# Zeroing the spare columns of VM earlier on GpSimd, in the prologue of a fused attention and mixer kernel

## The chip, the cores and the metric

The kernel runs on one core of one Trainium2 chip. The metric is device microseconds from start to end of one execution. A profile's span is some 1.8 us shorter than that time, because it counts from the first to the last instruction. Where two kernels are compared, they ran in turns on the same chip.

## The reference, cut to what matters

```python
x = A_x                                     # [1, 2048, 512] bf16
xn = _layernorm(x, axis=-1)
return x + _A_ref(xn, A_wqkv, A_wo) + _B_ref(xn, B_w1, B_b1, B_w2, B_b2)
# A: attention with 32 heads of 16; B: layer norm, token-mixing MLP, F = 1376
```

Only the first microseconds matter here. The layer norms of the first four token tiles (128 tokens each) must be done before the first scores can be computed, and all the rest follows.

## The kernel before

A list scheduler written in Python lays out every instruction of the five engines before the program is built. GpSimd ("pool") has several small jobs in the prologue. It takes the reciprocal root of each tile's variance, which VectorE ("dve") needs for the tile's layer norm, and it zeroes the columns of V and of VM (V scaled by a constant) that a later read touches beyond the written ones.

```python
def zero_memsets(nm, whole, kh):            # three of 128x256, one of 128x16
    for T in range(1, 4):
        sc.add("pool", lambda e, T=T: e.memset(kh[:, :, 8 * T, 0:16], 0.0), ...)
    sc.add("pool", lambda e: e.memset(whole[:, NKT * H * 17:], 0.0), ...)

def ln_rstd(t, n):                          # GpSimd: add epsilon, then power -1/2
    sc.add("pool", lambda e: e.tensor_scalar(mv[:, t:t + n, 3], mv[:, t:t + n, 1], EPS, None, ALU.add), ...)
    sc.add("pool", lambda e: e.tensor_tensor(mv[:, t:t + n, 2], ..., ALU.pow), ...)

def ln_norm(t):                             # VectorE: (x - mean) * root, bf16 to bf16
    sc.add(..., lambda e: e.tensor_scalar(xn_sb[:, t, :], x_sb[:, t, :], mv[:, t, 0:1], mv[:, t, 2:3],
                                          ALU.subtract, ALU.mult), ...)
# ... the prologue, in order:
zero_memsets("V", V17, v17_kh)
ln_sums(1)
warm_up(N_WARM, 5)                          # 13 matmuls that open TensorE's clock
ln_stats(0)
# ... statistics of tiles 1 and 2
ln_rstd(1, 2)
ln_norm(0)
ln_stats(3)                                 # ends with the root of tile 3 on GpSimd
for t in range(1, NPRE):
    ln_norm(t)
zero_memsets("VM", VM, vm_kh)               # on GpSimd: right behind the root of tile 3
# ... then TensorE transposes the normed tiles 0 to 3, projects Q and K, and scores begin
```

The softmax here doesn't subtract the row's maximum and nothing guards it: scores larger than these inputs give would overflow.

Of the kernel before, what the change touches and what calls it, by code (L numbers as in the profile page):

```python
# [52 lines left out]
SEM = 0.05  # L53
PE_SWITCH = 0.10
PER_LIST = 16
SEG = 8
RULES = (
    (0.5, 0.5, 0.3, 0.0, 6, 0),
    (0.3, 0.5, 0.3, 0.0, 6, 0),
# [6 lines left out]
    (0.5, 0.5, 0.3, 0.0, 4, 6),  # L66
    (0.5, 0.8, 0.45, 0.1, 4, -6),
)
RULE_OF = "00008220310000100058660800426859400150020974970367941473943140809177076731670813606801617338009600085119008766223163090020510000"
LN2_AT = 12  # L70
PIECE_OPEN = 1
HOLD_MAX = 2.0
ZERO_AT = 4
POOL_NORM = ()
STATS_LEAD = 0
N_LAST = 0
# [283 lines left out]
def bass_parallel_sum__softmax_full_mha__mixer_token_mlp__prompt_kernel(  # L360
# [18 lines left out]
    with ExitStack() as es:  # L379
        block = es.enter_context(nc.Block())  # L380

        def sb(name, shape, dt):
            return es.enter_context(nc.sbuf_tensor(name, shape, dt))
# [20 lines left out]
        VM = sb("VM", [128, NKT * H * 17 + 16], BF16)  # L404
# [37 lines left out]
        def bank(i):  # L442
            return ps[:, i * 512:(i + 1) * 512]
# [26 lines left out]
        vm_kh = VM[:, 0:NKT * H * 17].rearrange("p (k h c) -> p k h c", k=NKT, c=17)  # L470
# [8 lines left out]
        def zero_memsets(nm, whole, kh):  # L479
            for T in range(1, 4):  # L480
                sc.add("pool", lambda e, T=T: e.memset(kh[:, :, 8 * T, 0:16], 0.0),
                       writes=[(nm, t, T) for t in range(NT)], cost=(0.3, 0.4))
            sc.add("pool", lambda e: e.memset(whole[:, NKT * H * 17:], 0.0), writes=[(nm, NKT, 0)], cost=(0.1, 0.2))
# [56 lines left out]
        def ln_stats(t):  # L540
            sc.add("dve", lambda e: e.bn_stats(stats[:, t, :], x_sb[:, t, :]),
                   reads=[("x", t)], writes=[("stats", t)], cost=(0.6, 0.69))
            sc.add("dve", lambda e: e.bn_aggr(mv[:, t, 0:2], stats[:, t, :]),
                   reads=[("stats", t)], writes=[("mv", t)], cost=(0.12, 0.18))
            ln_rstd(t, 1)
# [8 lines left out]
        def ln_sums(t):  # L554

            for fn, col in ((ACTF.Identity, 3), (ACTF.Square, 1)):
                sc.add("act", lambda e, fn=fn, col=col: e.activation(xn_sb[:, t, :], x_sb[:, t, :], fn,
                                                                    accum_out=mv[:, t, col:col + 1]),
                       reads=[("x", t)], writes=[("xn", t), ("mv", t)], cost=(0.55, 0.7))
# [10 lines left out]
        def ln_norm(t):  # L570
            pool = t in POOL_NORM
            sc.add("pool" if pool else "dve", lambda e: e.tensor_scalar(xn_sb[:, t, :], x_sb[:, t, :], mv[:, t, 0:1], mv[:, t, 2:3],
                                                    ALU.subtract, ALU.mult),
                   reads=[("x", t), ("mv", t)], writes=[("xn", t)], cost=(2.09, 2.2) if pool else (0.3, 0.39), port=pool)
# [92 lines left out]
        def warm_up(n, bk, src=pT[:, NPB - 1, 0:512], keys=(("pT", NPB - 1),)):  # L667
            for _ in range(n):
                sc.add("pe", lambda e: e.matmul(bank(bk), lhsT=src[:, 0:128], rhs=src, start=True, stop=True),  # L669
                       reads=keys, writes=[("bank", bk)], cost=("F", (0, 1, 2, 3), 0.3), name="warm")  # L670

        sc.add("act", lambda e: e.activation(rcomp[:, 0, 0:1], mhalf[:], ACTF.Exp), reads=[("mhalf",)],
               writes=[("rcomp", 0)], cost=(1.4, 1.5))
        zero_memsets("V", V17, v17_kh)
        ln_sums(1)
        warm_up(N_WARM, 5)
        ln_stats(0)
# [5 lines left out]
        ln_stats(3)  # L683
        for t in range(1, NPRE):
            ln_norm(t)
        zero_memsets("VM", VM, vm_kh)

        TB = (0, 1, 2, 3)
        for t in range(NPRE):
# [18 lines left out]
        for half in (1, 0):  # L708
            cs = slice(256 * half, 256 * half + 256)
            sc.add("dve", lambda e, half=half, cs=cs: e.tensor_scalar(QT[:, 1, cs], bank(QB[half])[:, cs], qmask[:, 1:2], None, ALU.mult),  # L710
                   reads=[("bank", QB[half]), ("qmask",)], writes=[("QT", 1, r) for r in range(4)], cost=(0.35, 0.42))
        ln_norm(NPRE)
        for t in range(NPRE + 1, NPRE + 1 + STATS_LEAD):
            ln_stats(t)

        def zero_wo_t():
            dma("sp", wo_t[:], QT[:, 3:4, :].to_broadcast([128, 4, 512]),
                reads=[("QT", 3, r) for r in range(4)], writes=[("wo_t", z) for z in range(4)], name="zero")

        def block0_work(period):  # L720
            if period == ZERO_AT:
                zero_wo_t()
            if period == 0:
                for t in range(NPRE):
                    vt_tile_pe(t, 0, 5, t)
                vt_evac(list(range(NPRE)), 0, 5, "dve")

            def ok(t):
                return NPRE <= t < NT

            if ok(period + 2):
                transpose_copy(period + 2, 4, "dve")
            if ok(period + 1):
                kt_tile_evac(0, period + 1, EX_BANK, "dve")
            if ok(period) and period % 2 == 0:
                vt_evac([period, period + 1], 0, 5, "dve")
            if period == 1:
                warm_up(5, PV_BANK, KT[:, 0, 0:512], [("KTt", 0, z) for z in range(4)])
            if NKT - 2 <= period < PER_LIST:
                warm_up(3, 4, KT[:, 0, 0:512], [("KTt", 0, z) for z in range(4)])  # L740
            if ok(period + 3):
                transpose_pe(period + 3, 4)
            if ok(period + 2):
                kt_tile_pe(0, period + 2, EX_BANK)
                vt_tile_pe(period + 2, 0, 5, period % 2)
            if ok(period + 5 + STATS_LEAD):
                ln_stats(period + 5 + STATS_LEAD)
            if ok(period + 5) and period + 5 in POOL_NORM:
                ln_norm(period + 5)
            if ok(period + 4) and period and period + 4 not in POOL_NORM:  # L750
                ln_norm(period + 4)
            if period == 1:
                sc.add("pool", lambda e: e.memset(QT[:, 2:4, :], 0.0),
                       writes=[("QT", i, r) for i in (2, 3) for r in range(4)], cost=(0.9, 1.0))
# [644 lines left out]
        while True:  # L1399
            D_LATE, D_BACK, D_STEAL, PAIR_WAIT, piece_min, LATE_BY = RULES[int(RULE_OF[min(next_n, NN - 1) // SEG])]  # L1400
            cands = []
# [294 lines left out]
```

## Time and profile before

| | before |
|---|---|
| time, median of the first 3 runs | 684.36 us (684.14 to 684.39) |
| span of the profile | 682.6 us |
| TensorE / ScalarE busy | 98% / 98% |
| VectorE / GpSimd busy | 90% / 61% |
| norm of tile 3 on VectorE | 0.92 us, the other fifteen about 0.4 |
| first exponential on ScalarE | 11.33 us |

The lines behind this table stand in the prediction. Below, "norm 3" is VectorE's layer norm of token tile 3, and "load" is TensorE's weight load (PEld in the profile). In the profile's lines, x8 stands for eight instructions in one row, and a bracket tells how long the engine was idle before, and whose work ended that.

### The profile page before, as it was taken

The numbers are of one execution on the slowest core, as the hardware profiler recorded it, in microseconds if no ns is written. First come the engines' busy times: TensorE is split into PE (matmuls) and PEld (weight loads), VectorE is DVE, ScalarE is ACT, GpSimd is POOL, SyncE is SP. The second block draws the span as 40 slices with busy tenths as digits, with TensorE's granted clock in tenths as the row PEclk, the third lists the DMA queues.
The fourth block names the chain that finished last, engine by engine and source line by source line (L and its number), as shares of the span: only waits on it lengthen the run. The fifth ranks groups of instructions, "written<-read, shape, count | busy, mean of one in ns | idle before, by whom it ended". The sixth has DMA issues, their size and how long they took to land.

```text
span 682.6 us, 29520 instructions
## 1 busy us (share of the span) xinstructions
PE 670.7 (98%) x12969; PEld 312.4 (46%) x12972; DVE 617.0 (90%) x882; ACT 667.7 (98%) x731; POOL 417.6 (61%) x717
## 2 busy tenths in 40 slices
PE   8999999999999999999999999999999999999997
PEld 4534544445444445444444444444444444444443
DVE  7989899899998898999899899999999999989887
ACT  6999999999999999999999999999999999999995
POOL 5536557476676653667566577765667576565552
PEclk9999999999999999999999999999999999999999
DMA  7502001221002200122211112222221222212211
GB/s 216 133 8 52 19 20 22 51 48 25 19 18 48 49 22 21 25 50 47 49 35 30 41 43 56 54 58 48 46 55 40 57 55 57 54 43 59 53 46 52
DMA packets 86256, 32.85 MB, mean 48 GB/s; under 512 B 67440, under 2 KB 86128, under 8 KB 86128
## 3 DMA queue, kind: packets, MB, share of 16 engines
q1 hardware_dynamic: 85696, 30.58, 19.7%
q8 instruction: 101, 1.65, 1.1%
q10 hardware_dynamic: 432, 0.39, 0.2%
q14 instruction: 27, 0.22, 0.1%
HBM read 21.76 MB, written 2.35 MB: 35 GB/s over the span
## 4 chain that ended last, share of the span: by engine, by line
PE 74%; ACT 21%; DVE 3%; issue 1%; POOL 1%; DVEq 0%
PE ps L843 29%; PE ps L776 27%; PE ps L874 14%; ACT pT L800 14%; ACT x_sb L800 6%; PE ps L928 2%; PE ps L669 1%; ACT gT_sb L985 1%; DVE hx L588 1%; DVE pT L811 1%; POOL mv L584 0%; PE ps L600 0%; DVE x_sb L811 0%; PE ps L613 0%; PE ps L882 0%
## 5 line engine op out<-in xcount | busy, mean ns | idle before, releaser
L800 ACT ACTIVATE pT<-ps 128x1024 bf16<-128x1024 f32 x488 | 486.4, 1136 | 2.2 <-PE ps L776 1.7
L811 DVE TENSOR_SCALAR pT<-ps 128x1024 int16<-128x1024 f32 x220 | 269.1, 1223 | 26.4 <-PE ps L776 17.6
L776 PE MATMUL ps<-QT,KT 32*128 32x512 bf16 x2048 | 283.4, 384 | 5.3 <-ACT pT L800 3.2
L817 POOL INT64_ADD pT<-pT x342 | 207.0, 615 | 121.0 <-DVE pT L820 57.0
L843 PE MATMUL ps<-pT,V 128*32 128x256 bf16 x4696 | 242.1, 275 | 0.9 <-POOL pT L817 0.3
L800 ACT ACTIVATE x_sb<-ps 128x1024 bf16<-128x1024 f32 x223 | 241.8, 1142 | 0.2
L776 PEld LDWEIGHTS ps<-QT,KT 32*128 32x128 bf16 x2048 | 78.3, 91 | 179.7 <-ACT pT L800 67.3
L843 PEld LDWEIGHTS ps<-pT,V 128*32 128x32 bf16 x4696 | 111.6, 96 | 69.2 <-issue 55.3
L811 DVE TENSOR_SCALAR x_sb<-ps 128x1024 int16<-128x1024 f32 x93 | 113.6, 1222 | 9.8 <-PE ps L776 6.9
L817 POOL INT64_ADD pT<-x_sb x152 | 91.7, 614 | 48.5 <-DVE pT L820 28.6
L843 PE MATMUL ps<-x_sb,V 128*32 128x256 bf16 x1904 | 120.8, 275 | 0.0
L817 POOL INT64_ADD x_sb<-pT x120 | 73.3, 615 | 44.8 <-DVE pT L820 26.0
L843 PE MATMUL ps<-pT,VM 128*32 128x256 bf16 x920 | 63.7, 275 | 0.0
L820 DVE TENSOR_SCALAR pT<-pT 128x1024 int16<-128x1024 int16 x138 | 58.2, 424 | 3.9
L843 PEld LDWEIGHTS ps<-x_sb,V 128*32 128x32 bf16 x1904 | 49.5, 96 | 25.0 <-issue 20.8
L874 PE MATMUL ps<-gT_sb,wblk 128*32 128x512 bf16 (+1 forms) x704 | 57.9, 384 | 0.0
L874 PE MATMUL ps<-hx,wblk 128*32 128x512 bf16 x598 | 52.5, 383 | 0.1
L817 POOL INT64_ADD x_sb<-x_sb x44 | 27.0, 616 | 18.1 <-DVE pT L820 11.6
L882 PE MATMUL ps<-hx,wblk 32*128 32x512 bf16 (+1 forms) x92 | 35.6, 386 | 0.0
L843 PEld LDWEIGHTS ps<-pT,VM 128*32 128x32 bf16 x920 | 24.2, 96 | 12.9 <-issue 12.2
L820 DVE TENSOR_SCALAR pT<-x_sb 128x1024 int16<-128x1024 int16 x64 | 27.0, 425 | 1.9
L820 DVE TENSOR_SCALAR x_sb<-pT 128x1024 int16<-128x1024 int16 x60 | 25.6, 427 | 1.7
(105 smaller groups left out, 442.4 us busy)
## 6 DMA issues: line engine op xcount, KB each, us to landing
wblk<-in_B_w_dram SPq DMA_DIRECT2D x10, 512.0 KB, 4.5
wblk<-in_B_w_dram SPq DMA_DIRECT2D x16, 320.0 KB, 3.6
oC<-OT SPq DMA_DIRECT2D x248, 16.0 KB, 1.8
denb<-rden_scratch SPq DMA_DIRECT2D x124, 32.0 KB, 2.0
xr<-in_A_x_dram SPq DMA_DIRECT2D x16, 128.0 KB, 2.9
dcomp<-OT SPq DMA_DIRECT2D x124, 2.0 KB, 1.8
QT<-Qall SPq DMA_DIRECT2D x120, 16.0 KB, 1.8
out_dram<-osb SPq DMA_DIRECT2D x14, 128.0 KB, 2.0
```

The costliest lines, as they stand in the source:

```text
L588: return [dict(eng="dve", fn=lambda e: e.tensor_scalar(xn_sb[:, t, :], xn_sb[:, t, :], mv[:, t, 3:4], None, ALU.mult), reads=[("xn", t), ( ...
L669: sc.add("pe", lambda e: e.matmul(bank(bk), lhsT=src[:, 0:128], rhs=src, start=True, stop=True), reads=keys, writes=[("bank", bk)], cost=( ...
L776: specs.append(dict(eng="pe", fn=lambda e, r=r, bk=bk: e.matmul(bank(bk), lhsT=KT[32 * r:32 * r + 32, T, 128 * kt:128 * (kt + 1)], rhs=QT[ ...
L800: return [dict(eng="act", fn=lambda e: e.activation(buf(pbuf[n]), ps[:, s_ * 1024:(s_ + 1) * 1024], ACTF.Exp, scale=LN2_128), reads=[("ban ...
L811: return dict(eng="dve", fn=lambda e: e.tensor_scalar(buf_i(w), ps[:, s_ * 1024:(s_ + 1) * 1024], IBIAS, 0.0, ALU.add, ALU.max), reads=[(" ...
L817: return dict(eng=eng, fn=lambda e: e.int64_add(buf_i(o).bitcast(I64), buf_i(w).bitcast(I64), SHIFTS[k] * 0x0001000100010001), reads=[("pT ...
L820: return dict(eng=eng, fn=lambda e: e.tensor_scalar(buf_i(o), buf_i(w), float(SHIFTS[k]), 1.0, ALU.add, ALU.mult), reads=[("pT", w)], writ ...
L843: specs.append(dict(eng="pe", fn=lambda e, c=c, h=h, i=i, off=off: e.matmul(bank(PV_BANK)[32 * c:32 * c + 32, 256 * par:256 * par + 256], ...
L874: specs.append(dict(eng="pe", fn=lambda e, c=c, w=w: e.matmul(bank(EX_BANK)[32 * c:32 * c + w, :], lhsT=lhs_of(32 * c, 32 * c + w), rhs=rh ...
L882: return [dict(eng="pe", fn=lambda e: e.matmul(bank(EX_BANK)[0:dst_rows, :], lhsT=lhs_of(0, dst_rows)[rs], rhs=rhs[rs], start=begin, stop= ...
L928: return [dict(eng="pe", fn=lambda e, ct=ct, c=c: e.matmul(bank(EX_BANK)[32 * c:32 * c + 32, 128 * i:128 * (i + 1)], lhsT=xnT[:, ct, 128 * ...
L985: yield "act", [dict(eng="act", fn=lambda e, ap=ap: e.activation(ap, ap, ACTF.Gelu_apprx_tanh), reads=[("gT", f) for f in fts], writes=[(" ...
```

## The change

The intent is to do the zeroing of VM in a gap in which GpSimd waits for the first tile's statistics anyway, and not between the roots of tile 3 and tile 4.

```diff
-SEG = 8
+SEG = 4
-RULE_OF = "00008220310000100058..."      # 128 digits
+RULE_OF = "0000000088222200331100..."    # 256 digits, every old digit twice
+VM_EARLY = True
         zero_memsets("V", V17, v17_kh)
+        if VM_EARLY:
+            zero_memsets("VM", VM, vm_kh)
         ln_sums(1)
...
         for t in range(1, NPRE):
             ln_norm(t)
-        zero_memsets("VM", VM, vm_kh)
...
+        if not VM_EARLY:
+            zero_memsets("VM", VM, vm_kh)
         ln_norm(NPRE)
```

More of the change, by code (lines that the diff above doesn't have):

```diff
@@ L68 @@
 )
-RULE_OF = "00008220310000100058660800426859400150020974970367941473943140809177076731670813606801617338009600085119008766223163090020510000"
+RULE_OF = "0000000088222200331100000000110000005588666600880000442266885599440000115500002200997744997700336677994411447733994433114400880099117777007766773311667700881133660066880011661177333388000099660000008855111199000088776666222233116633009900002200551100000000"
 LN2_AT = 12
```

## The prediction

> **What bounds the kernel now.** I read the page first (busy shares, then the chain that ended last), then the order of instructions of both programs engine by engine, then the chain in order of time over the first 46 us, and last the timeline of all engines around the moved instructions. Two lines of the page:
>
> ```profile
> PE 670.7 (98%) x12969; PEld 312.4 (46%) x12972; DVE 617.0 (90%) x882; ACT 667.7 (98%) x731; POOL 417.6 (61%) x717
> ...
> PE 74%; ACT 21%; DVE 3%; issue 1%; POOL 1%; DVEq 0%
> ```
>
> The first is busy time by engine, the second the chain's share by engine. TensorE and ScalarE are both full for the whole span, and the chain alternates between them: scores, exponentials, products with V. GpSimd holds 1% of the chain, and that is one power of 2.97 us at 36.21 us, far from this change. So the body of some 640 us can gain nothing from an earlier memset. Only the prologue, up to the first exponential at 11.33 us, can, and whatever it gains or loses there is carried to the end once.
>
> The chain in order of time through the prologue (start, duration, what):
>
> ```profile
> 8.33 0.22 PE ps L613 x4
> 8.55 0.22 PE ps L600 x4
> 8.77 0.04 issue
> 8.81 0.40 PE ps L600 x4
> 9.21 0.22 PE ps L669
> 9.42 0.45 PE ps L651 x8
> 9.87 0.03 issue
> 9.90 0.40 PE ps L651 x4
> 10.29 0.67 PE ps L613 x12
> ```
>
> The transposes (L600) of token tile 2 end at 8.77, and those of tile 3 begin at 8.81 [...](0.40 for four matmuls instead of 0.22). What happened there, from the timeline of all engines:
>
> ```profile
> 7.21 0.58 POOL L551 TENSOR_TENSOR mv<-mv,mhalf 128x1 f32<-128x1 f32 x1
> ...
> 7.74 0.81 POOL L481 MEMSET VM<- 128x256 bf16 x3
> 7.83 0.92 DVE L572 TENSOR_SCALAR hx<-x_sb,mv 128x512 bf16<-128x512 bf16 x1 [0.18 <-POOL mv L551]
> ...
> 8.33 0.27 PEld L600 LDWEIGHTS ps<-ident,hx 128*128 128x128 bf16 x4
> ...
> 8.49 0.11 POOL L483 MEMSET VM<- 128x16 bf16 x1
> 8.81 0.23 PEld L600 LDWEIGHTS ps<-ident,hx 128*128 128x128 bf16 x4 [0.21 <-DVE hx L572]
> ```
>
> VectorE's layer norm of tile 3 starts at 7.83, 0.09 us behind the three VM memsets, and takes 0.92 us. TensorE's weight load for the tile 3 transposes then sits idle for 0.21 us, released by that norm (end 7.83 + 0.92 = 8.75). The group of that line shows how odd 0.92 is:
>
> ```profile
> L572 DVE TENSOR_SCALAR hx<-x_sb,mv x16: 379/394/924, 5.6 to 33.0; 128x512 bf16<-128x512 bf16 x16
> ```
>
> Sixteen norms of the same form, median 394 ns, one of 924 ns. The memsets that the change moves lie exactly on that one.
>
> **What the Trainium skill says.** "SBUF — State Buffer", section "Who interferes with whom": GpSimd's only SBUF ports are VectorE's second pair, whoever issues first holds the pair for its whole instruction and the other is blocked; a tensor_scalar can enter a two-port mode and contend, while a VectorE instruction with one SBUF input outside those modes doesn't. The trace agrees at 7.83: GpSimd was first, VectorE took 0.92 instead of 0.39. It doesn't agree everywhere: at 16.68 us a norm of the same form begins inside a GpSimd memset of 1024 columns (16.00 to 16.95) and takes an ordinary 0.41. So the lock explains the slow norm well, not certainly. "VectorE: DVE Perf Modes", section "What auto-detection actually checks": the fastest mode is taken for a single 16-bit source and a destination in SBUF; the norm has that form, and no field of the trace names the mode. "Perfetto Trace Analysis", section "GPSIMD Engine Instruction": spans of GpSimd are unreliable, so one takes start-to-start times. I do: the memsets have rows of 0.31 us but start every 0.25.
>
> **The change part by part.** The rule table first: the segment goes from 8 to 4 steps and the string from 128 to 256 digits. I compared them: the new string is the old one with every digit doubled, so every step gets the rule it had. That part is nothing. With line numbers stripped, the order of instructions is the same on TensorE, VectorE, ScalarE and SyncE, waits and buffer numbers included; on GpSimd alone three memsets of 128x256 and one of 128x16 move up by six instructions, in front of the reciprocal root of tile 0. Nothing is added or removed.
>
> What it puts in. GpSimd now:
>
> ```profile
> 2.73 0.82 POOL L481 MEMSET V<- 128x256 bf16 x3
> 3.48 0.11 POOL L483 MEMSET V<- 128x16 bf16 x1
> 4.42 0.26 POOL L549 TENSOR_SCALAR mv<-mv 128x1 f32<-128x1 f32 x1 [0.82 <-DVE mv L543]
> ```
>
> After V's memsets it is idle for 0.82 us, until VectorE delivers tile 0's moments. The VM group costs 3 x 0.25 + about 0.05 = 0.80 by start-to-start, so it runs from about 3.53 to 4.33, with its last row's end near 4.40. It fits with nothing over, so tile 0's root is late by 0 to 0.05. Behind it there is room: its power ends at 5.35, but VectorE only reaches norm 0 at 5.59 (the moments of tile 1 stand before it in order), and norm 0 ends at 6.00 while TensorE is in its 13 warm-up matmuls until about 6.7. Cost on the path: 0.
>
> What it takes away. GpSimd has nothing to do from 7.79 to 10.34 then, so those 0.80 us are worth nothing by themselves. But norm 3, started at 7.83 as before, should take 0.41 and end at 8.24 instead of 8.75. What of these 0.51 reaches the path: TensorE ends loading tile 2's weights at 8.33 + 0.27 = 8.60. Tile 3's load can then start at 8.60 instead of 8.81, so 0.21 is gained and 0.30 becomes slack.
>
> Does 0.21 survive? ScalarE's copy of tile 3 starts when its transposes end (9.24, from 9.21), now 9.03, and ends at 9.63 (0.60 long). The query projection of tile 3 (L651, 9.90) waits for that copy: now 9.69. Before it stand tiles 1 and 2 of L651; tile 2 needs VectorE's copy of 8.81 to 9.23, which waits for tile 2's transposes and doesn't move. Tile 1 ends issuing at about 9.28, so tile 2 starts at 9.28 without waiting, and its four are issued by 9.5. Then ScalarE's second query eviction (10.33, behind 10.29) comes at 10.12, TensorE's 12 key matmuls run without a gap, the scores start at 10.69 instead of 10.90 and the first exponential at 11.12 instead of 11.33. From there on, all the chain's links to 46 us are work behind work of this core, none a DMA arrival with a time of its own, so the rest shifts as it stands. Sum: 0 + 0 - 0.21 = -0.21 us, 684.36 to 684.15.
>
> **The rivals.** (a) The long norm is not the memsets' doing. For it: the ordinary norm at 16.68 beside a memset. Against: one outlier among 16, and it lies on the memsets. Then the time is unchanged, 684.36. (b) The port is taken elsewhere: at 3.5 to 4.4 the memsets now lie beside VectorE's statistics of tiles 0 and 2 (3.42 to 4.91). If these are blocked, norms 0 to 2 come up to 0.8 late, and since norm 1 (6.92) already leaves TensorE 0.26 idle at 7.39, up to 0.6 is lost: about 684.9. Against: the V memsets lay beside VectorE's memset of 2.84 without stretching it (0.48 for 512 elements), statistics beside the memset at 16.00 took 0.68, as they do everywhere, and the skill clears one-input work outside the two-port modes. (c) The gain is there but is met by something fixed in time, such as the query projection of tile 2 behind VectorE's unmoved copy: by my sum it clears it by some hundredths only, so half the gain, 0.1, could stay there: 684.25.
>
> **Range and chances.** I give the main line 70%, (a) 12%, (b) 5%, (c) 13%: 0.70 x -0.21 + 0.05 x 0.55 + 0.13 x -0.1 = -0.13. I name 684.2. Three runs of before spread over 0.25 us (684.14 to 684.39), more than the effect; with that on each side of the outcomes the range is 683.8 to 684.6. Two per cent is 13.7 us, more than the whole prologue up to the first exponential, and no instruction of the body changes place: 99% for the same.
>
> **What would show it.** Right: norm 3 at about 0.4 us, its longest row under 0.5; no idle time of TensorE's load before tile 3's transposes; VM's memsets from about 3.5; tile 0's root at 4.4 to 4.5; the first exponential near 11.12; later pieces of the chain all about 0.2 earlier. Wrong: a norm of 0.9 still there (a); statistics of 3.42 or 4.25 stretched past 0.7 and norm 1 later than 6.95 (b); the first exponential less than 0.15 earlier although norm 3 is short (c). Wrong altogether: a gain over 0.5 us, for which nothing in this profile has room.

## The result

| | before | after |
|---|---|---|
| time, median of 6 runs | 684.26 us (684.14 to 684.39) | 683.87 us (683.78 to 684.37) |
| ratio | | 0.9995 (95%: 0.9983 to 1.0008) |
| norm 3 | 0.92 us | 0.41 us |
| first exponential | 11.33 us | 10.70 us |
| span of the profile | 682.6 us | 682.2 us |

A ratio is the mean time of one kernel's runs over that of the other's in the same rounds, so it isn't quite the ratio of the medians. Its interval includes 1, so the ratio alone shows no gain. The single times say more: five of the six after (to 684.08) lie below the lowest of before (684.14).

The engines' busy shares on the page are those of before. TensorE's share of the chain went from 74% to 71%.

The timeline of the prologue after (start, duration, engine, line, what; lines of the file have moved by one: the norms are L573, the transposes L601):

```profile
3.53 0.81 POOL L482 MEMSET VM<- 128x256 bf16 x3
...
4.46 0.26 POOL L550 TENSOR_SCALAR mv<-mv 128x1 f32<-128x1 f32 x1
...
7.71 0.41 DVE L573 TENSOR_SCALAR hx<-x_sb,mv 128x512 bf16<-128x512 bf16 x1 [0.17 <-POOL mv L552]
...
7.90 0.51 PEld L601 LDWEIGHTS ps<-ident,hx 128*128 128x128 bf16 x8
```

The memsets run from 3.53, and GpSimd is at the root of tile 0 at 4.46. Norm 3 takes 0.41. TensorE loads the weights of the eight transposes of tiles 2 and 3 in one run (x8), with no idle time in between. The same place in the chain in order of time:

```profile
7.27 0.40 PE ps L601 x4
...
8.11 0.46 PE ps L601 x8
```

Before, tiles 2 and 3 took 0.22 + 0.04 + 0.40 = 0.66 us of the chain here (8.55 to 9.21). Now they take 0.46. That is 0.20, against the prediction's 0.21, at the predicted place. The group of the norms has lost its outlier:

```profile
L573 DVE TENSOR_SCALAR hx<-x_sb,mv x16: 380/393/414, 5.5 to 32.3; 128x512 bf16<-128x512 bf16 x16
```

**Where the time went.** ScalarE runs 726 activations in both traces, in the same order, so they can be paired by number. I worked these differences out from the two traces:

| ScalarE's activation number | start in before | after minus before |
|---|---|---|
| 16 | 18.21 us | -0.63 us |
| 211 | 199.39 us | -0.62 us |
| 391 | 364.48 us | -0.62 us |
| 706 | 655.93 us | -0.63 us |
| 726 (the last) | 679.30 us | -0.38 us |

The body runs in step over 640 us. All that was gained was gained before the first exponential, and 0.25 us was given back after 670 us. So two things had to be explained: why the prologue gained 0.63 and not 0.21, and what took 0.25 at the end.

The end is easily read. The timeline of the last normalisation on VectorE, first after, then before:

```profile
674.20 0.87 DVE L1099 TENSOR_TENSOR wkv_raw<-oC,denb 64x256 bf16<-64x256 f32 x2 [2.01 <-DMA oC<-OT]
675.00 0.70 DVE L1125 STREAM_TRANSPOSE denb<-ps 128x512 f32<-128x512 f32 x1
```

```profile
674.26 0.87 DVE L1095 TENSOR_TENSOR wkv_raw<-oC,denb 64x256 bf16<-64x256 f32 x2 [1.45 <-DMA oC<-OT]
675.36 0.72 DVE L1121 STREAM_TRANSPOSE denb<-ps 128x512 f32<-128x512 f32 x1 [0.23 <-PE ps L843]
```

The multiplication for an earlier block waits for a small transfer and stands in front of the transpose of the last block. It started at about the same time in both runs (674.20 and 674.26), although everything else was 0.63 earlier. So the transpose, which in before waited for TensorE (released at its end of 675.34), waited in the profile after for the multiplication. This transfer doesn't come equally late in every run. In the profile of the first experiment below, VectorE waited for TensorE again, and the 0.33 us that its body had gained was there to the end.

In the prologue, the 0.63 splits by the two timelines into three parts. The statistics of tile 0 started at 3.31 instead of 3.42 us, and norm 1 at 6.80 instead of 6.92, because x arrived earlier: 0.12. From norm 1 to the first exponential are 3.90 instead of 4.41 us: 0.51. Of that, 0.20 is the place just shown. The other 0.31 is the query projection of tile 0, 0.54 behind the start of tile 1's transposes before (7.93 and 7.39) and 0.23 after (7.50 and 7.27). Before, it waited for ScalarE's copy of tile 0, which came late because TensorE hadn't left its warm-up matmuls until 6.70. After, TensorE was at tile 0 at 5.97. Nothing in the change touches the warm-up.

### The profile page after: what moved, and what is told of

Read it like the earlier page. It is cut to its first block, busy times and chain, and to the rows that moved or that the text cites. A ratio compares the mean times of both kernels' runs of the same rounds, so it can differ in the third digit from the quotient of the medians.

```text
span 682.2 us, 29520 instructions
## 1 busy us (share of the span) xinstructions
PE 669.6 (98%) x12969; PEld 312.1 (46%) x12972; DVE 616.5 (90%) x882; ACT 667.7 (98%) x731; POOL 417.6 (61%) x717
## 4 chain that ended last, share of the span: by engine, by line
PE 71%; ACT 21%; DVE 3%; issue 2%; POOL 1%; SPq 1%; DMA 1%; DVEq 0%
PE ps L847 28%; PE ps L780 26%; ACT pT L804 14%; PE ps L878 14%; ACT x_sb L804 6%; PE ps L932 2%; ACT gT_sb L989 1%; DVE pT L815 1%; DVE hx L589 1%; SPq L458 1%; DMA oC<-OT 1%; POOL mv L585 0%; PE ps L601 0%; DVE x_sb L815 0%; PE ps L614 0%
```

## The experiments

**Theory.** The VM memsets held the port that GpSimd shares with VectorE, which stretched norm 3. That is all the mechanism. About the size: the kernel before is held at tile 3 by norm 3 whenever TensorE gets out of its warm-up, while the changed kernel is as early as TensorE lets it be. So the gain is small in a run where TensorE comes late, as in the one profile that the prediction read, and larger in others. **Rivals.** The gain could lie in filling GpSimd's early gap, in the rule table, or be a fixed 0.2 with chance for the rest.

### The move alone, with the old rule table

```diff
         zero_memsets("V", V17, v17_kh)
+        zero_memsets("VM", VM, vm_kh)
...
-        zero_memsets("VM", VM, vm_kh)       # behind the norms; SEG and RULE_OF as before
```

> The kernel before with only the move of the VM memsets; segment length and rule string as they were. Its instruction order equals that of the changed kernel on all five engines. My theory: the rule table is nothing, so this is a replicate of the change: norm 3 at 0.41 us, the load of tile 3's transposes right behind tile 2's, ratio about 0.9995 (0.2 to 0.5 us faster). Second theory, about the size: the 0.21 us of the prediction holds only when the TensorE clock gate opens late, as in the profile of before (the transposes of tile 0 began at 6.70 there, at 5.97 in the profile after); in an early run the tile 3 transposes gain about 0.5. Then the times fall into two groups about 0.3 us apart, with the kernel before in one group. Rival: the rule table matters somewhere I didn't see; then this one is 684.26.

Measured: 683.93 us (683.82 to 684.13, 5 runs) against 684.42 of before (9 runs, 684.27 to 685.07), ratio 0.9991 (0.9978 to 1.0005). The order of instructions is that of the changed kernel, and the gain is there, so the rule table does nothing. TensorE came late in this profile, as in that of before:

```profile
6.70 0.39 PE L600 MATMUL ps<-ident,hx 128*128 128x128 bf16 x4
...
7.83 0.41 DVE L572 TENSOR_SCALAR hx<-x_sb,mv 128x512 bf16<-128x512 bf16 x1 [0.18 <-POOL mv L551]
8.19 0.49 PEld L600 LDWEIGHTS ps<-ident,hx 128*128 128x128 bf16 x8
```

The first exponential starts at 10.97, 0.36 before that of the kernel before. All five times lie below all nine of before, though the interval of the ratio includes 1. Two groups of times 0.3 us apart, which the second theory expected, can't be told in five runs.

### The memsets behind the root of tile 4

```diff
-VM_EARLY = True
+VM_EARLY = False
```

> The changed kernel with its switch off: the VM memsets go behind the root of tile 4 (about 11 us), neither beside norm 3 nor into the early gap of GpSimd. Theory 1 (the memsets stretched norm 3, all the gain is in taking them away from it): norm 3 at 0.41 us, the time equals that of the changed kernel within 0.1 us (about 683.9). Rival (the gain is in GpSimd's early gap being filled, or in an order that starts the first roots differently): no gain, 684.26. A third outcome: at 11 us they meet the norm of tile 4 (12.39 in before, later start possible) and stretch that one to 0.9; then part of the gain is lost.

```profile
7.86 0.41 DVE L573 TENSOR_SCALAR hx<-x_sb,mv 128x512 bf16<-128x512 bf16 x1 [0.17 <-POOL mv L552]
...
11.11 0.80 POOL L482 MEMSET VM<- 128x256 bf16 x3
```

Measured: 683.85 us (683.80 to 684.37), ratio 0.9993 (0.9980 to 1.0005). GpSimd's early gap is empty again, the memsets run at 11.11, norm 3 takes 0.41 and norm 4 at 12.12 takes 0.40. The median is that of the changed kernel, and within 0.1 of that of the move alone in the same rounds. So by the medians filling the gap is worth nothing, and taking the memsets away from norm 3 is worth all. Theory 1 was right, and the third outcome didn't come. The execution with the profile was the longest of the five (684.37 us): its first exponential came 0.27 earlier than in the profile of before, and 0.21 of that was lost at the end, to the same transfer as in the profile after.

### Nine more memsets at the old place

```diff
         zero_memsets("VM", VM, vm_kh)
+        for T in range(1, 4):
+            for c in range(1, 4):            # parts of KT that are written much later
+                dst = KT[:, T, 512*c:512*(c+1)].rearrange("p (k x) -> p k x", x=32)[:, :, 0:16]
+                sc.add("pool", lambda e, dst=dst: e.memset(dst, 0.0), ...)
```

> The kernel before with nine more memsets of 128x256 (16 runs of 16 columns, into parts of KT that are written much later) directly behind the VM memsets, none of which waits for anything. Theory A (GpSimd holds the port until its run of memsets ends): GpSimd is busy to about 10.8 us, norm 3 ends near 11.05 instead of 8.75, its row is some 3.2 us long, and the time is longer by about 2.3 us (686.5). Theory B (the port changes hands at the end of one memset, so that VectorE waits for one to three of them): norm 3 stays at 0.9 us or less, the time stays within 0.2 us of before. Theory C (not the memsets): norm 3 at 0.92 as before.

```profile
8.04 3.20 DVE L572 TENSOR_SCALAR hx<-x_sb,mv 128x512 bf16<-128x512 bf16 x1 [0.17 <-POOL mv L551]
...
8.75 2.34 POOL L690 MEMSET KT<- 128x256 bf16 x9
11.29 0.23 PEld L600 LDWEIGHTS ps<-ident,hx 128*128 128x128 bf16 x4 [2.80 <-DVE hx L572]
```

Norm 3 lasted 3.20 us and ended at 11.24, 0.15 behind the last memset (8.75 + 2.34 = 11.09). The norm wasn't let in between the thirteen memsets, and all the delay reached the path: the exponentials are 2.48 us later than in the profile of before, 0.21 of it because norm 3 itself started later here. Theory A, in its mechanism and in the length of the row. The time was 687.21 us (686.68 to 687.70), above the 686.5 expected. Two of its four runs were almost 1 us longer than the other two. Their mean granted clock is 0.998 on record, against 1.000. Why is left open.

### One memset without gaps at the old place

```diff
         for t in range(1, NPRE):
             ln_norm(t)
+        sc.add("pool", lambda e: e.memset(QT[:, 2:4, :], 0.0), ...)   # 128x1024, VM still early
```

> The changed kernel with one memset of 128x1024 columns without gaps (the one at 16.00 us once more, an early copy of it) at the place that the VM memsets had, behind the root of tile 3. At 16.68 a norm beside this memset was not stretched. Theory A (any GpSimd memset that starts first blocks the norm until it ends): norm 3 is held to about 8.66 and its row is 0.9 to 1.2 us, time as before or up to 0.2 longer. Theory B (a memset without gaps doesn't block, one of many short runs does): norm 3 at 0.41, time as the changed kernel.

```profile
7.71 0.95 POOL L689 MEMSET QT<- 128x1024 bf16 x1
...
7.79 1.01 DVE L573 TENSOR_SCALAR hx<-x_sb,mv 128x512 bf16<-128x512 bf16 x1 [0.17 <-POOL mv L552]
```

Theory A again: the norm is held to 8.80, 0.14 behind the memset's end, and the time is 684.52 us (684.39 to 684.56), as before. So the gain goes when another memset takes the place, and the columns' layout isn't the cause. What the runs show is that a GpSimd memset under way holds the norm. That it does so through the shared port is what the page named in the prediction says; no field of the trace names the port. This also resolves the line that the prediction held against the lock. The same memset and a norm at 16 us in the kernel before:

```profile
16.00 0.95 POOL L753 MEMSET QT<- 128x1024 bf16 x1
16.68 0.41 DVE L572 TENSOR_SCALAR hx<-x_sb,mv 128x512 bf16<-128x512 bf16 x1
```

That norm ended at 17.09, 0.14 behind the memset's 16.95. A norm of 0.41 that starts 0.27 before the memset's end would end there anyway. So this norm doesn't speak against the lock. The next two runs test the reading.

### One and two memsets left at the old place

The blocked norms gave a rule: the end is the last memset's end plus 0.15, or the ordinary 0.41 behind the start, whichever is later. These two runs were to break it.

```diff
         zero_memsets("V", V17, v17_kh)
+        zero_memsets("VM", VM, vm_kh, (1, 2), True)         # the others; (1,) with two left
...
-        zero_memsets("VM", VM, vm_kh)                       # all three behind the root of tile 3
+        zero_memsets("VM", VM, vm_kh, (3,), False)          # one left; (2, 3) for two left
```

> The kernel before with two of the three VM memsets (and the short one) moved up and one left behind the root of tile 3. Rule under test, read from four blocked norms: norm 3 ends 0.15 us after the last memset's row does, since it needs the port only for its last part; otherwise it ends 0.41 after its start. One memset left ends about 0.31 after its start near 7.75, so 8.06, and 8.06 + 0.15 = 8.21 lies before the ordinary end of 8.24: norm 3 stays at about 0.41, the time is that of the changed kernel (683.8 to 684.1). Rival (a norm that finds GpSimd at work waits first and then needs its whole 0.41): norm 3 ends near 8.47, 0.64 long.

```profile
7.63 0.31 POOL L481 MEMSET VM<- 128x256 bf16 x1
7.72 0.41 DVE L573 TENSOR_SCALAR hx<-x_sb,mv 128x512 bf16<-128x512 bf16 x1 [0.17 <-POOL mv L552]
```

> The same with two memsets left. Their last row ends near 8.31, so by the rule norm 3 ends at about 8.46 and is some 0.62 long. The transposes of tile 3 then wait for it in a run with an early clock (load at about 8.5, against 8.2 of the changed kernel and 8.8 of before) and not in a late one; the time lies between the two kernels, 683.9 to 684.2. Rival (whole 0.41 after the memsets): norm 3 ends near 8.72, 0.9 long, time as before.

```profile
7.77 0.56 POOL L481 MEMSET VM<- 128x256 bf16 x2
7.85 0.62 DVE L573 TENSOR_SCALAR hx<-x_sb,mv 128x512 bf16<-128x512 bf16 x1 [0.17 <-POOL mv L552]
```

With one left, norm 3 takes 0.41, although the memset started first and lies over its first half (to 7.94). With two left it takes 0.62, as the rule says, tile 3's load waits for it until 8.53, and the first exponential came at 11.05. The rival's 0.64 and 0.9 are out. The times were taken on a chip where all three kernels ran longer: 684.58 us (683.74 to 684.76) and 684.72 (684.60 to 684.82) against 685.03 of before (684.60 to 685.19). So both lie above the times expected (at most 684.1 and 684.2), as before lies above its 684.26. The ratios are 0.9991 (0.9976 to 1.0006) and 0.9994 (0.9978 to 1.0011). The order is the expected one, and the intervals don't separate the two. The trace with one left is that of its fastest run by 0.75 us. In the trace with two left, the 0.27 us gained by the first exponential was lost over the body (ScalarE's activation 706 came 0.24 later than in before). No other profile drifts by as much, and the cause is open. The norms can be read from these two, the gain in time can't.

### Fewer and more warm-up matmuls

These four runs test the theory about the size. Only the number of warm-up matmuls differs from the two kernels.

```diff
-N_WARM = 13
+N_WARM = 11        # and 16
```

> The kernel before with 11 instead of 13 warm-up matmuls, nothing else different in the order of any engine. The theory under test is about the size: in the kernel before, the transposes of tile 3 wait for norm 3 (end 8.75) however early TensorE is free, so the time stays as before within 0.1 us (684.3 to 684.4), and tile 0's transposes begin at about 6.0. Rival (the gain is a fixed 0.21 and the rest of the 0.4 to 0.5 measured is chance between runs): warm-ups act on both kernels alike.

> The changed kernel with 11 warm-up matmuls. Theory: TensorE is free by 5.9 in every run, the clock gate's phase delays tile 0 no more, and the full gain of about 0.5 shows against the kernel before with 11 (683.8), with less spread than with 13. Rival: the difference to the kernel before with 11 is 0.2. A risk for both: with fewer warm-ups the clock may open later and the transposes run slowly; then both lose alike.

> The kernel before with 16 warm-up matmuls: TensorE is free between about 6.3 and 8.0 us, by when the clock opens. Theory: norm 3 hides part of that, since its end at 8.75 gates the transposes of tile 3 anyway; the time is 684.3 to 684.9.

> The changed kernel with 16 warm-up matmuls. Theory: TensorE itself, not the norm, is what comes last at tile 3, so the gain over the kernel before with 16 shrinks to 0 to 0.25 us, and the time is above the changed kernel's 683.9. Rival (gain fixed): the difference to the kernel before with 16 is the same 0.4 to 0.5 as with 13.

With 11, TensorE is at tile 0 at about 6.0 in both kernels (6.08 and 5.96). In the kernel before it then waits at tile 3 (first line), in the changed one it doesn't (second):

```profile
8.77 0.23 PEld L600 LDWEIGHTS ps<-ident,hx 128*128 128x128 bf16 x4 [0.47 <-DVE hx L572]
```

```profile
7.92 0.50 PEld L601 LDWEIGHTS ps<-ident,hx 128*128 128x128 bf16 x8
```

| | with 11 | with 16 |
|---|---|---|
| before | 684.38 us (684.27 to 684.46) | 684.33 us (684.25 to 684.44) |
| changed | 683.82 us (683.71 to 684.36) | 683.92 us (683.77 to 684.54) |
| difference of the medians | 0.56 | 0.41 |
| each one's ratio to the kernel before (684.27) | 1.0000 and 0.9993 | 1.0000 and 0.9996 |

The intervals of these ratios are about 0.0013 to each side, so the differences rest on the medians and, better, on the traces. The kernel before doesn't care how many warm-ups it has, as the theory says. With 11 the gain is the full 0.5. The smaller spread that was expected didn't come (0.65 us, against 0.59 with 13), so that TensorE is early in every run with 11 isn't shown. With 16 the 0 to 0.25 us that was expected didn't come either: the medians show 0.41, the number of the rival. Still the pair settles nothing. In the profiled run of the changed kernel TensorE was at tile 0 at 6.30 in spite of the 16, so it wasn't late there. Two of that kernel's five runs took 684.50 and 684.54, the other three 683.77 to 683.92, and only one of the five has a profile that I could read.

All profiles together, those with a stretched norm 3 first, each group in the order of the moment at which TensorE began tile 0 (all in us; the fourth column is the time for which the load was idle before tile 3):

| kernel | norm 3 | tile 0's transposes | idle | first exponential | from norm 1's start | from norm 3's end |
|---|---|---|---|---|---|---|
| before, 11 warm-ups | 0.86 | 6.08 | 0.47 | 11.29 | 4.35 | 2.57 |
| two memsets left | 0.62 | 6.26 | 0.22 | 11.05 | 4.10 | 2.57 |
| contiguous memset | 1.01 | 6.46 | 0.61 | 11.38 | 4.50 | 2.57 |
| before | 0.92 | 6.70 | 0.21 | 11.33 | 4.41 | 2.57 |
| nine more memsets | 3.20 | 6.70 | 2.80 | 13.81 | 6.68 | 2.57 |
| before, 16 warm-ups | 0.92 | 7.01 | 0.09 | 11.36 | 4.40 | 2.57 |
| changed, 11 warm-ups | 0.41 | 5.96 | 0.01 | 10.72 | 3.90 | 2.57 |
| changed | 0.41 | 5.97 | 0.01 | 10.70 | 3.90 | 2.57 |
| changed, 16 warm-ups | 0.41 | 6.30 | 0.01 | 10.73 | 3.89 | 2.57 |
| one memset left | 0.41 | 6.33 | 0.01 | 10.71 | 3.89 | 2.57 |
| the move alone | 0.41 | 6.70 | 0 | 10.97 | 4.05 | 2.72 |
| memsets at 11 us | 0.41 | 6.70 | 0 | 11.06 | 4.11 | 2.78 |

In all six profiles with a stretched norm 3, the first exponential comes 2.57 us behind the end of that norm, wherever TensorE stands. With a short norm it is 2.57 again where TensorE is at tile 0 by 6.33: there all of the 0.5 us by which the norm is shorter reaches the path. Where TensorE comes at 6.70, it is TensorE that comes last (2.72 and 2.78), and counted from norm 1 the gain is 0.36 and 0.30. Of these, 0.21 is the prediction's sum. The rest (0.15 and 0.09) is TensorE's: its query projection of tile 0 began 1.01 us behind norm 1 in the profile of before, and 0.86 and 0.92 behind it in these two. Nor is 0.21 the least. In the kernel before with 16 warm-ups, with TensorE at tile 0 at 7.01, the load was idle for only 0.09 us before tile 3, and the move could have gained no more than about that.

Why TensorE comes early or late isn't in the change. The Trainium skill ("TensorE: Matmul & The Clock Gate", section "What's actually happening") says that a gate halves the clock until a free-running activity window of 3413 ns was busy, so that the moment varies from run to run. The traces agree: their record of the granted clock begins at 7.02 us in the profile of before, 6.70 in the move alone and 5.22 in the profile after, and it stays at full clock for 675.84 us in each of the three, which is 198 such windows (198 or 199 in all twelve profiles). Until then the warm-ups' loads stand 0.43 us apart, and behind it in the profile after 0.21 us (5.33 and 5.54).

No version came out that beats the changed kernel: 11 warm-ups with it (683.82 us) lie within the spread of its own runs.

## Why the prediction was right or wrong

The time, 683.87 us, lies inside the range, near its low end, and the change is within 2% as foretold. The main line was 0.21 us of gain. The medians showed 0.39, and 0.49 for the move alone in the next series of runs. The range was made wide by the spread of single runs, and it holds the unchanged 684.36 of rival (a) too. So the time inside it decides little, and what follows rests on the traces.

- **The rule table is nothing**: right, shown by the move alone.
- **The cost of the earlier place is 0**: right. The memsets ran from 3.53 as worked out, and the root of tile 0 came at 4.46. That was 0.25 us behind VectorE's moments of tile 0, against 0.09 before, so the root was late by 0.16 and not by 0 to 0.05; norm 0 didn't wait for it. It fits the other way too: with the early gap empty the time is the same.
- **Norm 3 goes from 0.92 to 0.41**: right, and it is the memsets' doing, shown by removing them to two places, by lengthening them and by replacing them. Rival (a) is out.
- **Statistics blocked at 3.5 to 4.4, rival (b)**: out. The two that lay beside the moved memsets took 0.69 and 0.70, against 0.69 and 0.66 before.
- **"0.21 is gained and 0.30 becomes slack"**: this is the step that was mis-sized. The prediction took TensorE's 8.60, the end of tile 2's load, as given. That moment held for one run, in which the warm-ups had held TensorE until 6.70. In a run where TensorE is early, tile 2's load ends 0.3 us sooner: in the kernel before with 11 warm-ups it ended at 8.04 + 0.26 = 8.30 and TensorE then sat idle for 0.47 us. For the run that it read the sum was right (0.21 in the two profiles with TensorE at 6.70, once TensorE's own part is taken off). So the term is 0.09 to 0.5, by the run (the table above), and most runs seem to be nearer its upper end, as the medians show. Rival (c), half of the gain lost to VectorE's copy, had the sign wrong.
- **The first exponential near 11.12**: it was 10.97 and 11.06 in profiles with a late TensorE, 10.70 to 10.73 in the others. The prediction saw no room in its profile for a gain over 0.5 us; in the profile after it was 0.63 at the first exponential, of which 0.12 was x arriving earlier.
- **The rest shifts as it stands**: right for 640 us, to within 0.02 in the profile after (the trace with two memsets left drifted, see there). It wasn't right for the end in every run: in the profile after, a late transfer took 0.25 back. The prediction had looked for waits with a time of their own only up to 46 us.

## What to carry to other kernels

A long row of an instruction that is elsewhere short can be worth more than the wait that it causes in one profile: here one norm of sixteen pointed at the two engines' shared port. When a wait is removed, the gain is bounded by the next wait in parallel to it, and that one has to be read over several runs if it varies by run, as TensorE's start did. A last transfer or a fixed moment at the end can take part of a shift back, so the whole chain is to be read for it and not only the stretch where the change lies.

## What the Trainium skill lacked or had wrong

- "SBUF — State Buffer", section "Who interferes with whom": it says that the loser is blocked for the other's whole instruction. The runs add two things that it doesn't state. A run of thirteen GpSimd memsets in a row held VectorE through all of them (a 0.41 us norm took 3.20). That isn't a law: in the kernel before with 11 warm-ups VectorE got in behind the third memset, its norm took 0.86, and the short fourth memset took 0.25 instead of 0.11. And the blocked norm ended 0.14 to 0.15 us after the row of the memset that held it in all six profiles with one, which fits a norm whose first 0.25 us pass beside the memset: an overlap of 0.22 us cost nothing (0.41 with one memset left, 0.62 with two).
- "Perfetto Trace Analysis", section "GPSIMD Engine Instruction": it says that instructions that read no tensor have a single point in time. Memsets read none, and have rows of 0.31 us (256 columns) and 0.95 us (1024 columns) here. Its advice to go by start-to-start held: 0.25 us each.
- "GPSIMD Engine Reference", section "Common operations": it names the memset without a cost. Here it is 0.25 us for 256 bf16 columns and 0.92 us for 1024 (16.00 to the next instruction at 16.92), start to start.
